# A planner's table of costs is changed, and its order is searched with random shakes of the priorities: attention and two MoE layers on one core

## The chip, the core and the metric

The kernel runs on one core of one Trainium2 chip. The time is device microseconds for one execution of the whole program; less is better. Rows of a profile come from one execution recorded by the hardware profiler.

## What is computed

```python
def _attn_ref(q, k, v, tau):              # q, k, v: 4 batches, 8 heads, 576 positions, 64 wide
    scores = (1 / sqrt(64)) * matmul(q, k.transpose(0, 1, 3, 2))
    thresh = max(scores, axis=-1) - tau
    scores = where(scores >= thresh, scores, -1e9)
    attn = exp(scores - max(scores)); attn = attn / (sum(attn) + 1e-09)
    return matmul(attn, v)

x = attn_out.transpose(0, 2, 1, 3).reshape(2304, 512)
h = x @ w_in                               # 512 -> 2048
x = (h * clip(h + 3, 0, 6) / 6) @ w_out    # 2048 -> 512
h = x @ w2_in
out = (h * sigmoid(1.702 * h)) @ w2_out
```

## The kernel before, in words

**The stages.** Sixteen attention units (4 batches, 4 pairs of heads each) come first, and the first half of the first MoE layer is worked in between them (`moe_a`). Then follow the second half of that layer (`moe_b`) and the second layer (`moe2`), which streams the saved half of its weights back from DRAM. A matmul of nearly full float32 precision is made of three passes over a high and a low part.

**A unit of attention.** The unit loads K and Q of each of its two heads (tile `qk`, lines 545 and 546) and its values V (line 559). ScalarE copies K and Q into rounded high parts (tile `kqv`, line 366), GpSimd makes the low parts (line 369). TensorE forms nine score tiles of 128 rows (`ps`; line 573 from the fifth unit on, 589 and 605 before). For each, VectorE takes the row maximum (line 621), ScalarE the exponential (line 626, tile `e`), VectorE the threshold mask and sum (line 627). The result is transposed: on TensorE (line 678) with a ScalarE copy into tile `et` (line 681), or, in the last two batches, by `blocks`: VectorE transposes 32x32 blocks into `tr` (line 699), one DMA writes them to DRAM (line 702, `turned`, 1 MB) and four DMAs of 256 KB read them back into `et` (line 704). These four are called the block reads below. Then thirty value products on TensorE (line 756) multiply by V. TensorE's hidden and output matmuls of the first layer are lines 815 and 835 (835 serves the second layer too), the hidden matmuls of the second layer line 972.

**What sets the order.** All of this is recorded as operations with a cost in nanoseconds, what they read and write, and a nominal time. `Plan.order` is a list scheduler: it walks through time and gives each engine, when it is free, the ready operation with the smallest key; DMAs go through one queue in the order in which they become ready. `latest` runs the same backward and gives new keys. `settle` alternates the two. The resulting order is what each engine's instruction stream gets; it is fixed when the program is built, and on the chip each engine executes its own stream in that order and waits where an input is not there. SP issues all the data DMAs named here, from one stream. Where the plan sees TensorE idle and a bank of PSUM free, `fill` puts in dummy matmuls (line 1135, tile `two`), which compute nothing that is used.

The search is in `settle`. Its first loop is always run; the second runs once for each number in `KICKS`, the tuple that is empty before:

```python
        for seed in KICKS:
            self.order(kicked(key, length, seed))
            key = self.latest()
            length = self.order(key)
```

`kicked` draws from the seed a stretch of the plan and a size (100 to 3000 ns), and adds Gaussian noise of that size to the keys in that stretch.

Of the kernel before, what the change touches and what calls it, by code (L numbers as in the profile page):

```python
# [18 lines left out]
P = 128  # L19


PE, ACT, DVE, POOL, SP, DMA = range(6)
# [8 lines left out]

PORT = {DVE: {"W", "XHB", "XLB", "XD", "XLC", "GT2", "GL"}, POOL: {"kl", "qs", "ql", "vl", "W", "GD", "N", "RM", "EL", "XL", "XLC", "GL"}}

KICKS = ()


class Buf:
# [23 lines left out]
class Plan:  # L61
# [158 lines left out]
    def settle(self):  # L220
# [3 lines left out]
        for _ in range(3):  # L224
# [4 lines that stand above are left out]
# [24 lines left out]
def kicked(key, length, seed):  # L253

    rng = random.Random(seed)
    size, width = rng.choice((100.0, 300.0, 1000.0, 3000.0)), rng.choice((2e4, 6e4, 2e5, 2e6))
    lo = rng.uniform(-length - width / 2, 0.0)
    return [k + rng.gauss(0.0, size) if lo <= k < lo + width else k for k in key]
# [3 lines left out]
def tile_top_attention_moe_moe2(  # L262
# [13 lines left out]
    nc = tc.nc  # L276
    B, H, _, S = q2.shape
    DM, DFF = w1i.shape
# [40 lines left out]
    def add(eng, cost, time, name, fn, rd=(), wr=(), touch=()):  # L319
        op = pl.add(eng, cost, time, fn, rd, wr, name, touch)  # L320
        for c, names in changed:
            if any(b.pool in names for b in op.bufs):
                op.deps.add(c)
        return op

    def move(time, name, nbytes, fn, rd=(), wr=()):

        op = add(SP, 590, time, name, fn, rd, wr)
        add(DMA, nbytes / 360, time, name, lambda: None, rd, wr).deps.add(op)

    def buf(tag, ring, pool, shape, dt=F32):
        return Buf(pl, tag, ring, lambda: pools[pool].tile(shape, dt, tag=tag, name=tag, bufs=ring), pool)

    def bank(cls):
        b = Buf(pl, "pm", 1, lambda: pools["pm"].tile([P, 512], F32, tag=f"pm{b.bank}", name="pm"), "pm")
        b.cls = cls
        return b
# [9 lines left out]
    def f32(ap):  # L347
        return ap.bitcast(F32)

    def pe(n):  # L350
        return 7 + 0.43 * n

    def act(n):
        return 51 + 0.834 * n

    def dve(n):
        return 69 + 1.042 * n
# [7 lines left out]
    def copy(o, i, **kw):  # L365
        return lambda: nc.scalar.activation(out=o(), in_=i(), func=ACTF.Copy, **kw)  # L366
# [121 lines left out]
    ets = [buf("et", 1, "et", [P, 10 * S]) for _ in range(2)]  # L488

    def et_a(et, p, hd, k):  # L490
        o = (0, 2560)[p] + (5 * hd + k) * CH[p][1]
        return et.t[:, o:o + CH[p][1]]
# [7 lines left out]
    def et_p(p):  # L500
        return ets[1].t[:, 2560 * p:2560 * p + 2048].rearrange("p (h k n) -> p h k n", h=2, k=4)

    def et_4(p):
        return ets[1].t[:, 2560 * p + 2048:2560 * p + 2560].rearrange("p (h n) -> p h n", h=2)

    def et_r():
        return ets[1].t[:, 5120:].rearrange("p (h k n) -> p h k n", h=2, k=5)
# [4 lines left out]
    def unit(u, b, j, t0):  # L512
# [4 lines left out]
        def K(name, s=0):  # L517
            return t0 + 2700 * s + NOMINAL[name]
# [4 lines left out]
        def tile_():  # L523
            return buf("kqv", 12, "st", [P, QC], F32R)

        if early:
            khb, qhb, qzb = tile_(), tile_(), buf("g", HF, "gp", [P, 640], F32R)
            for hd in range(2):
                r, o = slice(64 * hd, 64 * hd + 64), slice(64 - 64 * hd, P - 64 * hd)
# [24 lines left out]
        vs = tile_()  # L554

        def v_(k, hd):
            return f32(vs.t).rearrange("p (k h d) -> p k h d", k=5, h=2)[:, k, hd, :]
# [3 lines left out]
        xrs = {p: buf(f"xr{p}", 2, "xr", [P, CH[p][1]]) for p in range(2)}  # L561
# [20 lines left out]
        def score1(s):  # L582

            ps, (hd, m) = buf("ps", 2, "ps", [P, 2, 512]), tiles[s]
            q0 = 256 * hd + m * P

            def mm():
                for i in range(2):
                    nc.tensor.matmul(ps.t[:, i, :SH], f32(qzb.t)[:, q0:q0 + P], f32(khb.t)[:, i * SH:(i + 1) * SH], start=True, stop=True)

            add(PE, 4 * 243, K("S", s), "S", mm, [(qzb, x) for x in (("z", hd), (hd, 0))] + [khb], [ps])
            soft(s, ps)

        def score(ss):

            if len(ss) == 1 and tiles[ss[0]] is not None:
                return score1(ss[0])
            pss = {s: buf("ps", 2, "ps", [P, 2, 512]) for s in ss}

            def mm():  # L600
                for i in range(2):
                    for s in ss:
                        t = tiles[s]
                        rows, q0 = (slice(0, P), 256) if t is None else (slice(64 * t[0], 64 * t[0] + 64), t[1] * P - 256)
                        nc.tensor.matmul(pss[s].t[:, i, :SH], f32(qhb.t)[rows, q0:q0 + P], f32(khb.t)[rows, i * SH:(i + 1) * SH], start=True, stop=True)

            add(PE, 4 * 243 + 300 + 40 * (len(ss) > 1), K("S", ss[0]), "S", mm, [qhb, khb], [pss[s] for s in ss])
            for s in ss:
                soft(s, pss[s])

# [72 lines left out]
        def last_keys(p, ss):  # L683
            trans([(s, 4, tiles[s][0] * 256 + tiles[s][1] % 2 * P) for s in ss], 512, lambda kn: (et_4(p)[:kn], lambda x: x.rearrange("p (h n) -> p h n", h=2)), ets[1], (p, 4), ss[-1])
# [9 lines left out]
        def blocks(p, ss):  # L694

            et, at, src = ets[1], ss[-1], buf("tr", 1, "tr", [P, 4, 2, 4, 2, 32])
            for s in ss:
                hd, t = tiles[s]
                add(DVE, dve(512), K("DT", s), "DT", lambda hd=hd, t=t % 2, e=e_of[s]: nc.vector.transpose(out=src.t[:, :, hd, :, t, :].rearrange("p g k j -> p k g j"), in_=e.t[:, :512].rearrange("p (k g j) -> p k g j", k=4, g=4)),
                    [e_of[s]], [(src, s)])  # L700
            turned, there = turns[p]
            move(K("DM", at), "DM", 16 * P * 512, lambda: nc.sync.dma_start(out=turned, in_=src.t.rearrange("p g h k t j -> p (g h k t j)")), [src], [there])
            for g in range(4):
                move(K("DM", at) + 3000, "DM", 4 * P * 512, lambda g=g: nc.sync.dma_start(out=ets[1].t[32 * g:32 * g + 32, 2560 * p:2560 * p + 2048].rearrange("p (a n) -> p a n", a=4),
                     in_=turned[:, 512 * g:512 * g + 512].rearrange("(a p) n -> p a n", a=4)), [there], [(et, ("m", p, g))])
            last_keys(p, ss)

# [21 lines left out]
        def av(p, at):  # L729

            n, xr, et, pv = CH[p][1], xrs[p], ets[0], bank(1)
            regions = [(p, hd, k) for hd in range(2) for k in (0, 2)] + [(p, 4), ("z", p)] + ["r", "r4"] * p

            def mm():
                for k in range(5):
                    for hd in range(2):
                        nc.tensor.matmul(pv.t[64 * hd:64 * hd + 64, :n], v_(k, hd), et_a(et, p, hd, k), start=k == 0, stop=k == 4)

            op = add(PE, 350 + 10 * (1 + 0.84 * n), K("AV", at), "AV", mm, [vs] + [(et, r) for r in regions], [pv], [xr])
            add(ACT, act(n), K("XR", at), "XR", copy(lambda: xr.t, lambda: pv.t[:, :n]), [pv], [xr])  # L740
            return op

        def av_(at):

            et, pv = ets[1], [bank(1), bank(1)]
            for x in pv:
                add(PE, 0, K("AV", at), "AV", lambda: None, [vs, et], [x], xrs.values())

            def mm():
                def x(p, k, hd):  # L750
                    return et_r()[:, hd, k] if p == 2 else et_4(p)[:, hd] if k == 4 else et_p(p)[:, hd, k] if b not in TURNED else et_m(p)[:, :, hd, k].rearrange("p a t j -> p t a j")

                for p, o, c, n in ((0, pv[0], 0, 256), (1, pv[0], 256, 256), (2, pv[1], 0, 64)):
                    for k in range(5):
                        for hd in range(2):
                            nc.tensor.matmul(o.t[64 * hd:64 * hd + 64, c:c + n], v_(k, hd), x(p, k, hd), start=k == 0, stop=k == 4)  # L756

            add(PE, 450 + 10 * (2 + 0.84 * S), K("AV", at), "AV", mm, [vs, et], pv, xrs.values())
            add(ACT, act(256), K("XR", at), "XR", copy(lambda: xrs[0].t, lambda: pv[0].t[:, :256]), [pv[0]], [xrs[0]])
            add(ACT, act(256), K("XR", at), "XR", copy(lambda: xrs[1].t[:, :256], lambda: pv[0].t[:, 256:]), [pv[0]], [(xrs[1], 0)])  # L760
            add(ACT, act(64), K("XR", at), "XR", copy(lambda: xrs[1].t[:, 256:], lambda: pv[1].t[:, :64]), [pv[1]], [(xrs[1], 1)])
# [432 lines left out]
```

## Time and profile before

| | us |
|---|---|
| median of 3 runs | 1097.37 (1097.24 to 1100.8) |
| the profiled execution | 1093.03 |
| its span, first to last instruction | 1091.2 |
| TensorE (PE) busy in the span | 1058.7 (97%) |
| VectorE, ScalarE, GpSimd busy | 724.2, 638.1, 515.3 |

TensorE is busy nearly all the time, the others are not. The profiled execution took 1.8 us more than its span, and was 4.3 us faster than the median of the runs. TensorE's busy time includes the dummy matmuls and matmuls that ran at a lower granted clock.

### The profile page before, as it was taken

How to read it: one execution, taken by the hardware profiler on the slowest of the kernel's cores; microseconds unless marked ns; L12 is line 12 of the kernel's file. 1: busy time of each engine (PE TensorE's matmuls, PEld its weight loads, DVE VectorE, ACT ScalarE, POOL GpSimd, SP SyncE). 2: the span in 40 equal slices, each digit the busy share in tenths (PEclk: the TensorE clock that was granted, in tenths of full speed). 3: DMA queues.
4: the chain of work that ended last, by engine and by line, in shares of the span. 5: the costliest groups of instructions: out<-in, count | busy, mean ns of one | idle time of the engine just before them, and what ended most of it. 6: DMA issues, size and time to landing. Idle time of an engine off the chain costs nothing.

```text
span 1091.2 us, 20840 instructions
## 1 busy us (share of the span) xinstructions
PE 1058.7 (97%) x7706; PEld 970.0 (89%) x7706; DVE 724.2 (66%) x1485; ACT 638.1 (58%) x1340; POOL 515.3 (47%) x598
## 2 busy tenths in 40 slices
PE   8999899989898999999999999999999999999998
PEld 7677788888787989999999999989998989889888
DVE  6998766676686784467877333778787675563634
ACT  4888777765576664576555324666566665444433
POOL 3679868675686764555466224541323332001000
PEclk9999999999999999999999999999999999999999
DMA  7334222266878687445654212435545543312202
GB/s 206 116 120 129 96 68 78 91 190 176 250 213 271 200 242 195 140 137 166 203 174 145 79 48 61 132 105 183 175 137 173 167 139 102 116 46 71 92 1 73
DMA packets 90053, 150.19 MB, mean 138 GB/s; under 512 B 8928, under 2 KB 51552, under 8 KB 87904
## 3 DMA queue, kind: packets, MB, share of 16 engines
q1 hardware_dynamic: 89952, 148.87, 44.8%
q8 instruction: 60, 0.98, 0.4%
q14 instruction: 41, 0.34, 0.1%
HBM read 101.52 MB, written 47.32 MB: 136 GB/s over the span
## 4 chain that ended last, share of the span: by engine, by line
PE 69%; DVE 9%; DMA 7%; ACT 5%; POOL 4%; issue 3%; SPq 2%; POOLq 0%; DVEq 0%; ACTq 0%
PE py L835 23%; PE pm L815 14%; PE pm L972 14%; PE pm L835 6%; PE pm L756 4%; PE ps L573 4%; PE pm L678 2%; DMA qk<-in_k_dram 2%; DVE e L627 2%; DMA qk<-in_q_dram 1%; ACT e L626 1%; DVE nm L621 1%; DMA wrawstg<-in_w1i_dram 1%; POOL e L640 1%; POOL kqv L369 1%
## 5 line engine op out<-in xcount | busy, mean ns | idle before, releaser
L835 PE MATMUL py<-g,outhring 128*128 128x512 f32 (+2 forms) x1152 | 287.7, 337 | 2.6 <-DVE g L369 1.3
L835 PEld LDWEIGHTS py<-g,outhring 128*128 128x128 f32 x1152 | 193.7, 188 | 20.6 <-DVE g L369 3.3
L835 PE MATMUL py<-g,outlring 128*128 128x512 f32 (+2 forms) x576 | 193.5, 336 | 0.0
L815 PE MATMUL pm<-xh,inhring 128*128 128x256 f32 (+1 forms) x512 | 154.8, 302 | 2.3 <-DVE t L827 2.2
L815 PE MATMUL pm<-xl,inhring 128*128 128x256 f32 (+1 forms) x512 | 151.8, 296 | 0.0
L815 PE MATMUL pm<-xh,inlring 128*128 128x256 f32 (+1 forms) x512 | 151.7, 296 | 0.0
L972 PE MATMUL pm<-outhring,inhring 128*128 128x256 f32 x512 | 144.5, 282 | 1.5 <-ACT u L366 0.8
L972 PE MATMUL pm<-outlring,inhring 128*128 128x256 f32 x512 | 143.6, 281 | 0.0
L972 PE MATMUL pm<-outhring,inlring 128*128 128x256 f32 x512 | 143.5, 280 | 0.0
L621 DVE TENSOR_REDUCE nm<-ps 128x1 f32<-128x576 f32 x144 | 106.2, 750 | 34.4 <-PE ps L573 30.3
L369 POOL TENSOR_TENSOR g<-t,g 128x256 fp32r<-128x256 f32 (+1 forms) x104 | 88.1, 851 | 82.7 <-ACT g L366 79.9
L627 DVE SCALAR_TENSOR_TENSOR e<-ps,th,e 128x576 f32<-128x576 f32 x128 | 102.6, 810 | 33.2 <-ACT e L626 31.9
L827 DVE SCALAR_TENSOR_TENSOR t<-t,pm 128x256 f32<-128x256 f32 (+1 forms) x128 | 57.1, 448 | 94.0 <-ACT t L826 93.7
L835 PEld LDWEIGHTS py<-g,outlring 128*128 128x128 f32 x576 | 108.2, 188 | 10.0
L369 POOL TENSOR_TENSOR wmstg<-wmstg,wrstg 128x512 uint32<-128x512 uint32 x48 | 64.6, 1347 | 94.8 <-DVE wmstg L422 77.3
L835 PE MATMUL pm<-g,outhring 128*128 128x256 f32 (+1 forms) x512 | 107.7, 301 | 0.5 <-POOL g L369 0.4
L369 POOL TENSOR_TENSOR g<-tc,g 128x512 fp32r<-128x512 f32 x24 | 31.8, 1326 | 161.6 <-ACT g L366 154.9
L826 ACT ACTIVATE t<-pm,half 128x256 f32<-128x256 f32 (+1 forms) x128 | 63.7, 498 | 74.3 <-PE pm L815 68.6
L626 ACT ACTIVATE e<-ps,nm 128x576 f32<-128x576 f32 x128 | 93.0, 733 | 15.2 <-DVE nm L621 13.4
L815 PEld LDWEIGHTS pm<-xh,inhring 128*128 128x128 f32 x512 | 98.0, 191 | 4.2 <-DVE t L827 2.9
L972 PEld LDWEIGHTS pm<-outhring,inhring 128*128 128x128 f32 x512 | 96.8, 189 | 4.9 <-ACT u L366 1.1
L972 PEld LDWEIGHTS pm<-outlring,inhring 128*128 128x128 f32 x512 | 96.9, 189 | 2.6
(114 smaller groups left out, 2433.8 us busy)
## 6 DMA issues: line engine op xcount, KB each, us to landing
turned<-tr SPq DMA_DIRECT2D x16, 1024.0 KB, 4.5
et<-turned SPq DMA_DIRECT2D x64, 256.0 KB, 5.6
wrawstg<-in_w1i_dram SPq DMA_DIRECT2D x16, 512.0 KB, 4.0
wrawstg<-in_w1o_dram SPq DMA_DIRECT2D x16, 512.0 KB, 3.8
wrawstg<-in_w2i_dram SPq DMA_DIRECT2D x16, 512.0 KB, 3.9
wrawstg<-in_w2o_dram SPq DMA_DIRECT2D x16, 512.0 KB, 3.9
qk<-in_k_dram SPq DMA_DIRECT2D x24, 288.0 KB, 3.9
qk<-in_q_dram SPq DMA_DIRECT2D x24, 288.0 KB, 3.7
```

Source lines behind the costliest of these rows:

```text
L369: return lambda: (nc.vector if eng == DVE else nc.gpsimd).tensor_tensor(out=o(), in0=a(), in1=b(), op=op)
L573: nc.tensor.matmul(ps.t[:, i, :SH], qss[hd].t[:, q0:q0 + P], w[hd].t[:, i * SH:(i + 1) * SH], start=a, stop=z)
L621: add(DVE, 665, K("R", s), "R", lambda: nc.vector.tensor_reduce(out=nm.t[:, c], in_=ps.t[:, :, :SH], op=ALU.max, axis=AX.XY, negate=True), ...
L626: add(ACT, 624, K("X", s), "X", lambda: nc.scalar.activation(out=ev(), in_=ps.t[:, :, :SH], func=ACTF.Exp, bias=nm.t[:, c]), [ps, (nm, s)] ...
L627: add(DVE, 729, K("M", s), "M", lambda: nc.vector.scalar_tensor_tensor(out=ev(), in0=ps.t[:, :, :SH], scalar=th.t[:, c], in1=ev(), op0=ALU ...
L678: nc.tensor.transpose(pt.t[:kn, o:o + P], e_of[s].t[:, keys(k)], id_b.t)
L756: nc.tensor.matmul(o.t[64 * hd:64 * hd + 64, c:c + n], v_(k, hd), x(p, k, hd), start=k == 0, stop=k == 4)
L815: nc.tensor.matmul(ph.t[:, :n], a, v, start=(cc == 0 and i == 0), stop=(cc == KC - 1 and i == 2))
L826: add(ACT, 93 + act(n), K("RL"), "RL", lambda: nc.scalar.activation(out=tt_(), in_=pt(), func=ACTF.Relu, scale=1.0 / 6.0, bias=half_b.t), ...
L827: add(DVE, dve(n), K("GT"), "GT", lambda: nc.vector.scalar_tensor_tensor(out=tt_(), in0=tt_(), scalar=1.0, in1=pt(), op0=ALU.min, op1=ALU. ...
L835: nc.tensor.matmul(py.t[:, :n], a, v, start=(st and i == 0), stop=(sp and i == 2))
L972: nc.tensor.matmul(o.t[:, :n], u.t[:, ws], v.t[:, xv], start=(st and kk == 0 and i == 0), stop=(sp and kk == 1 and i == 2), skip_group_che ...
```

## The change

Six numbers by which the plan counts durations are changed, and the tuple of seeds is filled with 14 numbers. No operation, buffer or transfer is added or taken away, apart from the dummy matmuls, whose number follows from the plan. Costs of matmuls go up a little (`pe`), those of value products and of the first units' scores down or up by up to 250 ns, and each block read is counted as 1274 ns of the DMA queue where it was 728 ns (7 and 4 times 128 x 512, divided by 360).

```diff
-KICKS = ()
+KICKS = (1, 3, 102, 147, 227, 262, 375, 1642, 1718, 1761, 2323, 3460, 4428, 4473)
...
     def pe(n):
-        return 7 + 0.43 * n
+        return 9 + 0.428 * n
...
-            add(PE, 4 * 243, K("S", s), "S", mm, [(qzb, x) for x in (("z", hd), (hd, 0))] + [khb], [ps])
+            add(PE, 4 * 243 + 60, K("S", s), "S", mm, [(qzb, x) for x in (("z", hd), (hd, 0))] + [khb], [ps])
...
-            add(PE, 4 * 243 + 300 + 40 * (len(ss) > 1), K("S", ss[0]), "S", mm, [qhb, khb], [pss[s] for s in ss])
+            add(PE, 4 * 243 + 200, K("S", ss[0]), "S", mm, [qhb, khb], [pss[s] for s in ss])
...
-                move(K("DM", at) + 3000, "DM", 4 * P * 512, lambda g=g: nc.sync.dma_start(out=ets[1].t[32 * g:32 * g + 32, 2560 * p:2560 * p + 2048].rearrange("p (a n) -> p a n", a=4),
+                move(K("DM", at) + 3000, "DM", 7 * P * 512, lambda g=g: nc.sync.dma_start(out=ets[1].t[32 * g:32 * g + 32, 2560 * p:2560 * p + 2048].rearrange("p (a n) -> p a n", a=4),
...
-            op = add(PE, 350 + 10 * (1 + 0.84 * n), K("AV", at), "AV", mm, [vs] + [(et, r) for r in regions], [pv], [xr])
+            op = add(PE, 150 + 10 * (1 + 0.84 * n), K("AV", at), "AV", mm, [vs] + [(et, r) for r in regions], [pv], [xr])
...
-            add(PE, 450 + 10 * (2 + 0.84 * S), K("AV", at), "AV", mm, [vs, et], pv, xrs.values())
+            add(PE, 200 + 10 * (2 + 0.84 * S), K("AV", at), "AV", mm, [vs, et], pv, xrs.values())
```

Nearly every stretch of every engine's stream stands in another order. Three places follow; names with numbers are single buffers, and the numbers differ between the two programs for the same thing.

**First place: SP's stream where the thirteenth unit's second K is loaded.** `in_k2`, `in_q2` and `in_vp` are K, Q and V in DRAM; K's load of the unit's second head is `qk_3842` before and `qk_3825` in the change. Before:

```order
L702 DMA turned_111<-tr_3665 128x2048
L704 DMA et_1647<-turned_111 32x4x512 x3
L546 DMA qk_3807<-in_q2_dram 128x576
L704 DMA et_1647<-turned_111 32x4x512
L559 DMA kqv_3790<-in_vp_dram 128x640
L545 DMA qk_3842<-in_k2_dram 128x576
L767 DMA x1d_99<-xr0_3826 128x256
```

The same place in the change:

```order
L704 DMA et_1502<-turned_111 32x4x512 x4
L546 DMA qk_3815<-in_q2_dram 128x576
L545 DMA qk_3825<-in_k2_dram 128x576
L559 DMA kqv_3795<-in_vp_dram 128x640
L704 DMA et_1502<-turned_112 32x4x512 x4
L546 DMA qk_3885<-in_q2_dram 128x576
```

K's load has moved ahead of V's, and still stands behind four block reads; four more block reads now follow directly.

**Second place: ScalarE's stream where this K is copied** (`kqv_3908<-qk_3842` before, `kqv_3951<-qk_3825` in the change); `t` and `g` belong to the first layer's gate, `e` and `er` to the softmax of the unit before. Before:

```order
L826 ACTIVATE t_3870<-pm_3819,half_110 128x320
L366 ACTIVATE g_3878<-t_3817 128x320
L623 ACTIVATE th_3850<-nm_3835,nt_108 128x1
L366 ACTIVATE kqv_3908<-qk_3842 128x576
L826 ACTIVATE t_3916<-pm_3866,half_110 128x320
L626 ACTIVATE e_3921<-ps_3852,nm_3835 128x576
L623 ACTIVATE th_3850<-nm_3835,nt_108 128x1
```

In the change:

```order
L626 ACTIVATE er_3928<-ps_3897,nm_3719 128x576
L623 ACTIVATE th_3724<-nm_3719,nt_108 128x1
L826 ACTIVATE t_3941<-pm_3881,half_110 128x320
L366 ACTIVATE kqv_3951<-qk_3825 128x576
L366 ACTIVATE kqv_3845<-qk_3815 128x576
L626 ACTIVATE e_3970<-ps_3943,nm_3719 128x576
L623 ACTIVATE th_3724<-nm_3719,nt_108 128x1
```

The copy of K stands later among the softmax pieces of the unit before it, and next to a copy of Q; a gate piece and softmax pieces still stand behind it.

**Third place: TensorE's stream where the fifteenth unit's scores begin.** Scores are line 573 (`kqv_4496,kqv_4536` before, `kqv_4488,kqv_4541` in the change), value products of an earlier unit line 756. Before:

```order
L756 MATMUL pm_4818<-et_1647,kqv_4174 64x256 x20
L756 MATMUL pm_4839<-et_1647,kqv_4174 64x64 x10
L835 MATMUL pm_4784<-g_4685,outhring1_1259 128x256 x2
L835 MATMUL pm_4784<-g_4685,outlring1_1279 128x256
L835 MATMUL pm_4784<-g_4737,outhring1_1358 128x256 x2
L835 MATMUL pm_4784<-g_4737,outlring1_1363 128x256
L835 MATMUL pm_4784<-g_4745,outhring1_1416 128x256 x2
L835 MATMUL pm_4784<-g_4745,outlring1_1440 128x256
L835 MATMUL pm_4784<-g_4807,outhring1_1530 128x256 x2
L835 MATMUL pm_4784<-g_4807,outlring1_1541 128x256
L573 MATMUL ps_4897<-kqv_4496,kqv_4536 128x288 x2
L573 MATMUL ps_4897<-kqv_4503,kqv_4536 128x288 x2
```

In the change:

```order
L573 MATMUL ps_4780<-kqv_4488,kqv_4541 128x288 x2
L573 MATMUL ps_4780<-kqv_4519,kqv_4541 128x288 x2
L756 MATMUL pm_4794<-et_1502,kqv_4125 64x256 x20
L756 MATMUL pm_4815<-et_1502,kqv_4125 64x64 x10
L678 MATMUL pm_4852<-id_103,e_4675 64x128
```

The first score of the new unit has moved ahead of the thirty value products. This order stands at the starts of four units in the change (the 12th, 14th, 15th and 16th) and of one before (the 11th).

The dummy matmuls (line 1135) are 65 before and 37 in the change; each leaves two records in a trace. Ahead of the first hidden matmul there are 36 and 25, from there to the last unit's value products 8 and 0, behind them in the first layer 4 and 10, in the second layer 17 and 2. Of the first 36 and 25, 22 and 21 stand ahead of the first transpose; 14 and 4 follow. VectorE's stream holds, ahead of the operation that the first hidden matmuls wait for last (the fourth unit's product with the reciprocal sums, `xr`), the same operations in both: 19 each of maximum, threshold and mask, and 19 of the weights' decoding.

## Rows read from the trace of the kernel before

**Rows 1.** The page's busy times: engine, us busy, share of the span, instructions.
```profile
PE 1058.7 (97%) x7706; PEld 970.0 (89%) x7706; DVE 724.2 (66%) x1485; ACT 638.1 (58%) x1340; POOL 515.3 (47%) x598
```

**Rows 2.** Windows by stage: stretch, length, busy us per engine, clock, DMA share, GB/s.
```profile
18.00:60.00 42.00, 38.24 (x261) 28.05 (x258) 37.96 (x95) 34.53 (x65) 23.71 (x29) 1.00 0.50 153
60.00:220.00 160.00, 154.56 (x1209) 132.68 (x1211) 119.16 (x291) 122.85 (x247) 127.61 (x164) 1.00 0.31 95
220.00:410.00 190.00, 176.50 (x1437) 160.61 (x1433) 143.70 (x307) 119.64 (x283) 131.05 (x184) 0.97 0.77 222
410.00:700.00 290.00, 288.80 (x2210) 284.73 (x2209) 163.82 (x322) 146.19 (x307) 145.07 (x139) 1.00 0.45 135
700.00:1080.00 380.00, 377.05 (x2455) 342.95 (x2455) 244.12 (x435) 205.64 (x426) 82.20 (x61) 1.00 0.35 115
```

**Rows 3.** Timeline of TensorE: start, us, instructions, [idle before and its releaser].
```profile
238.88 0.94 PE L678 MATMUL pm<-id,e 128*64 128x128 f32 x4 [2.03 <-ACT et L681]
...
277.06 1.30 PE L573 MATMUL ps<-kqv 128*128 128x288 f32 x4 [3.41 <-DVE e L627]
...
301.05 0.41 PE L815 MATMUL pm<-xh,inhring 128*128 128x320 f32 x1 [1.71 <-DVE t L827]
...
354.15 0.79 PE L573 MATMUL ps<-kqv 128*128 128x288 f32 x4 [2.99 <-DVE e L627]
```

**Rows 4.** The chain that ended last, and DMA issues: what led to these waits.
```profile
230.85 7.11 DMA qk<-in_k_dram
...
265.12 8.56 DMA qk<-in_q_dram
...
292.68 6.67 DMA qk<-in_k_dram
...
343.46 7.68 DMA qk<-in_k_dram
...
qk<-in_k_dram SPq DMA_DIRECT2D x24, 288.0 KB, 3.9
```

**Rows 5.** Timelines of SP and ScalarE ahead of the third wait.
```profile
292.01 0.38 SPq L559 DMA_DIRECT2D kqv<-in_vp_dram  x1
292.68 0.35 SPq L545 DMA_DIRECT2D qk<-in_k_dram  x1
...
299.38 0.68 ACT L366 ACTIVATE kqv<-qk 128x576 fp32r<-128x576 f32 x1 [3.69 <-DMA qk<-in_k_dram]
```

**Rows 6.** Windows of TensorE just behind the four waits: stretch, length, busy, clock, DMA, GB/s.
```profile
239.00:243.00 4.00, 4.00 (x22) 0.57 0.65 265
...
276.90:281.00 4.10, 3.94 (x20) 0.62 1.05 316
...
301.00:304.00 3.00, 2.92 (x18) 1.00 0.10 41
...
354.00:359.00 5.00, 4.85 (x26) 0.66 0.65 163
```

**Rows 7.** Block reads: the DMA issues, and a window that holds eight of them.
```profile
et<-turned SPq DMA_DIRECT2D x64, 256.0 KB, 5.6
...
262.00:276.00 14.00, 11.65 (x108) 1.00 1.00 234
```

**Rows 8.** Dummy matmuls: those from 0 to 60 us, those from 700 us, a timeline.
```profile
0.00:60.00 60.00, 11.68 (x72) 10.86 (x72) 1.00 0.53 157
...
L1135 PE MATMUL pm<-two x34: 270/275/275, 712.2 to 1017.6; 128*128 128x128 f32 x34
...
712.19 0.83 PE L1135 MATMUL pm<-two 128*128 128x128 f32 x6
712.78 0.48 PE L835 MATMUL py<-g,outhring 128*128 128x512 f32 x1
714.25 0.50 PE L835 MATMUL py<-g,outhring 128*128 128x512 f32 x1 [0.99 <-DVE g L369]
```

**Rows 9.** The chain: one unit's value products.
```profile
142.24 5.05 PE pm L756 x60
```

## The prediction, made before the changed kernel was run

> **What bounds the kernel now.** I read the page first. TensorE is busy 97% of the span, the next engine 66% [rows 1], and no work is added or removed, so the change can only win back what TensorE loses: idle time, dummy matmuls and half-clock stretches. The windows by stage say where that lies. Idle TensorE is the length less the busy time: 3.8 us from 18 to 60 us, 5.4 from 60 to 220, 13.5 from 220 to 410, 1.2 from 410 to 700, 3.0 from 700 to 1080 [rows 2]. The stretch from 220 to 410 holds half of it, and is the only one with a granted clock under 1.00 and the one with the busiest DMA (0.77). It is where attention goes through the block reads.
>
> The timeline of that stretch shows four waits that make up most of it: 2.03, 3.41, 1.71 and 2.99 us, sum 10.1 [rows 3]. The releaser named is ScalarE or VectorE, but the chain that ended last goes on behind them to a load of K or Q each time, which took 7.11, 8.56, 6.67 and 7.68 us from issue to landing, where K's median is 3.9 [rows 4]. The third shows the mechanism: SP issued V's load at 292.01 and K's at 292.68; ScalarE then stood 3.69 us until K came [rows 5], and everything behind that copy in ScalarE's stream, a gate piece and two softmax pieces, stood with it. TensorE waited for the gate piece.
>
> Each wait can cost twice. Behind the first, second and fourth the granted clock is 0.57, 0.62 and 0.66 over 4.0, 4.1 and 5.0 us with TensorE busy; behind the third, the shortest, it stayed at 1.00 [rows 6]. A clock of 0.57 over 4.0 us is 0.43 x 4.0 = 1.7 us lost; the others lose 0.38 x 4.1 = 1.6 and 0.34 x 5.0 = 1.7. Together 5.0 us, so late loads cost 10.1 + 5.0 = 15.1 us.
>
> **Why the loads are late.** The plan counted a block read of 256 KB as 728 ns. In a window that holds eight of them the DMA engines were full (share 1.00) and moved 234 GB/s [rows 7]: 262 KB (decimal) over 234 is 1.12 us. Four reads were thus undercounted by 4 x 0.39 = 1.6 us, and a group of four or eight stood ahead of each late load. The plan believed K was there when ScalarE's turn came. The new figure, 1.27 us, is near the traced one.
>
> **The change, part by part.** *Late loads.* A truer cost does not make a read faster; it can only let the plan move loads ahead, or put K's copy later so that less stands behind it. The streams show some of both. For the thirteenth unit K moves ahead of V's 320 KB, worth 328 / 234 = 1.4 us of DMA, of the 1.71 us wait; but four reads still stand ahead of it. ScalarE's copy stands behind more of the previous unit's softmax. Of the four loads two (13th and 15th unit) are moved ahead of V so; the other two keep their place behind reads. Bounds: nothing saved, or all 15.1. I take half, as two of four are moved on SP: **-7.6 us**.
>
> *Dummy matmuls of the second layer.* There are 34 records; six took 0.59 us from the first's start to the next matmul's (712.19 to 712.78), so 0.098 each and 3.3 in all [rows 8]. The change keeps 4 records, 0.4 us: 2.9 us less. What covers a loss here is nothing, as TensorE is the only busy engine; but a gap may come back as plain waiting, as in the 0.99 us just behind those six [rows 8]. Bounds 0 and -2.9; I take **-2.5**.
>
> *Dummy matmuls of the start.* 72 records become 50, at 0.098 us 2.2 us less. But from 18 to 60 us VectorE is busy 37.96 of 42.0 [rows 2], and its stream holds the same operations ahead of the first hidden matmul in both orders. TensorE would just stand where it now spins: **0**, bounds -2.2 and what the clock may cost (below). The middle ones, 16 records less before the last value products and 12 more behind them, cancel within half a us.
>
> *Cost figures of matmuls and value products.* A unit's value products took 5.05 us [rows 9]; the plan said 450 + 10 x (2 + 0.84 x 576) = 5308 ns and now says 5058. The figure is right now, but 0.25 us in each of twelve units is small beside gaps of 2 to 3 us. These and the smaller figures go together: 0.
>
> *The shaken order.* Idle time outside the four waits is 3.4 us in 220 to 410, 5.4 before it, 4.2 after it, 13 us in all [rows 2, 3]. The seeds reshuffle all of it, and I cannot price that from an order. Bounds: 5 us gained (a third or so) or 5 lost; I take **-1.5**, as the plan whose costs are nearer the traced ones should lose less to surprise.
>
> Sum: -7.6 - 2.5 + 0 + 0 - 1.5 = **-11.6 us**. From the profiled execution's 1093.0 that is 1081.4; it ran 4.3 us under the median of the runs, and I carry the difference to that: 1097.4 - 11.6 = 1085.8, so 1086.
>
> **The rivals.** *All waits go.* If K's copies now stand late enough everywhere, the late loads give 15.1, the dummies 2.9 and the shake 4: -22, about 1075. For it: the chain names one cause for all four. Against it: reads still stand ahead of most loads.
>
> *The DMA engines are the bound and nothing is won there.* They were full from 262 to 276 us [rows 7], and the same bytes must move; a load put ahead makes the block reads late, and with them the value products that wait for them. Then only the second layer's dummies and the shake remain: -2.5 - 1.5 = -4, but a read group pushed behind a load costs some of that; about 1094. Against it: the share over 220 to 410 is 0.77 [rows 2], so a quarter of the DMA time is free there. The Trainium skill has a rule that speaks for this rival (Perfetto Trace Analysis, What "DMA-bound" means): a kernel can be bound on the DMA engines themselves, and then large descriptors are what matter. By that rule an order of issue would give nothing here and the time would stay at about 1094; the trace agrees for 14 us of the stretch and not for all of it.
>
> *Slower: a score put ahead of the value products.* At four unit starts (one before) the new unit's first score now stands ahead of thirty value products in TensorE's stream. TensorE takes its matmuls in that order, so if K is late there, 5.05 us of work [rows 9] that may be ready stands behind the wait. If each of the four waits as long as the worst now (3.41 us) and drops the clock (1.7), that is 4 x 5.1 = 20.4 us; with the gains above kept, -11.6 + 20.4 = +8.8, so 1106. It decides the sign from 11.6 / 4 = 2.9 us per start. Against it: the plan now counts the reads ahead of K, and value products wait for block reads themselves, so they may not be ready earlier.
>
> *The clock falls at the start.* Fourteen dummies behind the first transpose become four. Three of the four waits above were followed by half clock, the one of 1.71 us was not [rows 3, 6]; idle gaps in place of dummies could do the same, at 1.6 to 1.7 us for each low stretch [rows 6]. Two such would give 1086 + 3.4 = 1089. Against it: VectorE ends most waits there, so a slower TensorE is partly hidden. The Trainium skill states it as a rule (TensorE: Matmul & The Clock Gate, Part 1): half clock is the default state, and activity releases it. By that rule fewer dummies could make the start slower, to the same 1089; the trace shows the clock at 1.00 there with all 36.
>
> **How the numbers follow.** Chances: the forecast 0.47 (its own range 1080 to 1091, from a quarter to all of the late loads with the small terms at either end), all waits gone 0.15, DMA-bound 0.22, slower 0.08, clock at the start 0.08. A measurement of this kernel can tell about 0.5%, 5.5 us, from no change: faster means under 1091.9, slower over 1102.9. Faster: 0.47 + 0.15 + 0.06 of the clock case + 0.01 of the DMA case = 0.69. Same: 0.20 + 0.02 = 0.22. Slower: 0.08 + 0.01 = 0.09. The range 1076 to 1098 takes in the forecast, the clock and the DMA case and the better part of the case in which all waits go; it leaves out the slower case and the tail of the best one.
>
> **What would show it.** Late loads: idle TensorE from 220 to 410 falls from 13.5 to about 8 us, the granted clock there rises from 0.97 towards 0.99, and ScalarE's waits for K and Q shrink; if the loads still take 7 us and more but no TensorE wait hangs on them, the copies' place did it, not SP's. Dummies: 4 records from 700 us on, and idle there not above 3 us. Start: the first hidden matmul (line 815) still at about 60 us, with more idle ahead of it. I am wrong if idle from 220 to 410 stays above 11 us, if new waits in line 573 stand right ahead of line 756, or if the gain sits mostly in the first 220 us.

## The result, and the profile after

The changed kernel takes 1084.28 us (median of 4 runs, 1079.79 to 1085.12) against 1098.61 for the kernel before (1097.24 to 1100.8, with one run more than was shown ahead of the prediction). The ratio is 0.9864, 95% interval 0.9833 to 0.9895: 14.3 us faster, inside the range of 1076 to 1098 and 1.7 us under the forecast of 1086.

The two profiled executions differ by less, 1085.12 against 1093.03, 7.9 us. The one of before was faster than its four runs, and the one of after was the slowest of its four. So the rows below show where time went, and the size of it is taken from the runs.

The windows by stage of the changed kernel, with the columns of [rows 2] (length, busy PE, PEld, DVE, ACT, POOL, granted clock, DMA share, GB/s):

```profile
18.00:60.00 42.00, 36.90 (x242) 26.18 (x241) 38.30 (x94) 34.50 (x67) 24.50 (x29) 1.00 0.51 151
60.00:220.00 160.00, 152.28 (x1174) 128.25 (x1175) 120.98 (x294) 124.35 (x245) 126.38 (x165) 0.98 0.31 93
220.00:410.00 190.00, 181.17 (x1503) 166.45 (x1500) 150.72 (x321) 125.66 (x299) 136.04 (x189) 1.00 0.82 231
410.00:700.00 290.00, 289.08 (x2212) 284.18 (x2211) 170.43 (x317) 143.31 (x298) 142.18 (x134) 1.00 0.45 133
700.00:1080.00 380.00, 377.55 (x2450) 342.87 (x2448) 244.11 (x433) 206.84 (x428) 81.24 (x60) 1.00 0.36 113
```

Length less busy, against [rows 2]: idle TensorE fell from 13.5 to 8.8 us in 220 to 410, where the clock rose from 0.97 to 1.00 (some 5 us of lost clock gone), and from 3.0 to 2.4 us from 700 on. It rose from 5.4 to 7.7 us in 60 to 220, where the clock fell from 1.00 to 0.98, worth 0.02 x 160 = 3.2 us. The gain sits where the prediction put it; part of it is given back before.

Who TensorE waited for in 220 to 410 us of the changed kernel (us in total, times, longest), the three largest:

```profile
PE pm L756 <- DVE t L827: 1.8, 2, 1.5
PE ps L573 <- DVE er L627: 1.7, 1, 1.7
PE ps L573 <- DVE e L627: 1.4, 2, 1.1
```

No wait is over 1.71 us, where before there were 2.03, 3.41, 1.71 and 2.99 [rows 3], and the clock is 1.00 in the whole stretch. How that came is seen at the first place of the order, the thirteenth unit's second K. Of the changed kernel, SP's timeline (start, length, what):

```profile
288.54 0.38 SPq L545 DMA_DIRECT2D qk<-in_k_dram  x1
```

ScalarE's:

```profile
297.42 1.26 ACT L366 ACTIVATE kqv<-qk 128x576 fp32r<-128x576 f32 x2 [3.20 <-DMA qk<-in_k_dram]
```

and TensorE's (in brackets the wait before, and for whom):

```profile
300.49 0.77 PE L573 MATMUL ps<-kqv 128*128 128x288 f32 x4 [1.11 <-DVE e L627]
```

K was issued at 288.54 and its copy began at 297.42: the load was not faster than before but slower, up to 8.9 us (6.67 then [rows 4]). ScalarE still stood 3.20 us for it, against 3.69 [rows 5]. But more of the unit before stood ahead of the copy in ScalarE's stream, and TensorE lost 1.11 us in place of 1.71. Over the stretch ScalarE's copies waited less for loads too. The view of the tile `qk` from 220 to 410 us says who waited for it; first the row of the kernel before:

```profile
  ACT kqv L366: 17.9, 7
```

and of the changed kernel:

```profile
  ACT kqv L366: 8.7, 4
```

The loads themselves became slower. Of the same views, the time of all loads of K and Q in the stretch, before and then in the change:

```profile
DMA to landing us min/median/max: 3.2/6.2/9.8
```

```profile
DMA to landing us min/median/max: 3.0/7.6/9.9
```

The median of 3.9 us for K [rows 4] is that of the whole execution. In this stretch a load took 6.2 us in the median before too, so the four late ones (6.67 to 8.56) did not stand far out. A block read also lands later, 7.4 us after issue in the median of the execution (5.6 before [rows 7]). The transfers are no faster; the waits for them are shorter.

### The profile page after: what moved, and what is told of

Read it like the earlier page. It is cut to its first block, busy times and chain, and to the rows that moved or that the text cites. A ratio compares the mean times of both kernels' runs of the same rounds, so it can differ in the third digit from the quotient of the medians.

```text
span 1083.3 us, 20735 instructions
## 1 busy us (share of the span) xinstructions
PE 1052.5 (97%) x7650; PEld 960.9 (89%) x7650; DVE 735.4 (68%) x1485; ACT 640.0 (59%) x1340; POOL 515.9 (48%) x598
```

## Experiments

Two theories stood against each other. Theory 1: true costs do it; the plan stops believing that K and Q are there when they queue behind block reads. Theory 2: the search does it; the seeds give a shorter order, whatever the figures. All ratios are against the kernel before on the same chip, with 95% intervals. There are three sets, each on a chip of its own: e1 to e4, e5 to e8, e9 to e12; between sets the ratios are compared.

### The six figures without the seeds (e1)

```diff
-KICKS = (1, 3, 102, 147, 227, 262, 375, 1642, 1718, 1761, 2323, 3460, 4428, 4473)
+KICKS = ()
```

> All six new cost figures, no seeds. Theory 1 (true costs: the plan stops believing that loads behind block reads are there, and that is where the 14 us come from) expects most of the gain, a ratio of 0.986 to 0.991, idle TensorE from 220 to 410 us at 9 us or less and the clock there at 0.99 or 1.00. Theory 2 (search: the seeds shorten the order, whatever the figures) expects 0.997 to 1.003, with waits of 2 to 3 us left behind late loads. Both in part: 0.991 to 0.997.

Measured: 1.0022 (1.0009 to 1.0035), 1099.52 us. The figures alone win nothing. Yet the late loads are gone: ScalarE's copies waited 2.2 us in all for `qk` in 220 to 410 us, where it was 17.9. Other waits stand in their place. Of e1, two windows and then the two largest waits of TensorE from 220 to 410 us:

```profile
220.00:410.00 190.00, 180.25 (x1472) 0.97 0.79 224
700.00:1080.00 380.00, 374.48 (x2415) 1.00 0.37 117
```

```profile
PE ps L573 <- DVE e L627: 3.9, 4, 1.8
PE pm L815 <- ACT et L681: 2.4, 2, 2.1
```

Idle time in 220 to 410 is 9.8 us, less than before, but the clock is as low as it was (0.97), and TensorE is idle for 5.5 us of the second layer in place of 3.0. So a short wait of ScalarE for its loads does not by itself make a kernel faster.

### The figure of the block reads alone (e2)

```diff
-                move(K("DM", at) + 3000, "DM", 4 * P * 512, lambda g=g: nc.sync.dma_start(out=ets[1].t[32 * g:32 * g + 32, 2560 * p:2560 * p + 2048].rearrange("p (a n) -> p a n", a=4),
+                move(K("DM", at) + 3000, "DM", 7 * P * 512, lambda g=g: nc.sync.dma_start(out=ets[1].t[32 * g:32 * g + 32, 2560 * p:2560 * p + 2048].rearrange("p (a n) -> p a n", a=4),
```

> The kernel before with one figure changed: a block read is counted as 1274 ns in place of 728. Theory 1 expects nearly as much as all figures together give, 0.987 to 0.993, since the late loads (10.1 us of waits and 5.0 us of clock) are the only large loss that a figure speaks of. Theory 2 expects 0.997 to 1.003.

Measured: 1.0071 (1.0048 to 1.0093), slower. Here too the copies waited less for `qk` (6.0 us). Theory 1 as stated has fallen: the one figure that speaks of the loss does not bring the time. The working put the other five figures at nothing; without a search they are worth 0.5% (1.0071 here, 1.0022 with all six in e1).

### The old figures with a search of their own (e3)

```diff
-KICKS = ()
+KICKS = (1, 11, 338, 1139, 1226, 1269, 1414, 4302)
```

> The kernel before with its own old figures and eight seeds kept by the same rule (a seed is kept if the plan gets shorter by the plan's own count) out of the first 6000. Theory 2 expects as much as the change gave, 0.984 to 0.991. Theory 1 expects the late loads still there (clock under 0.99 from 220 to 410 us, waits of 2 us and more behind copies of K and Q) and 0.994 to 1.003, since a plan with reads counted at 728 ns gets shorter on paper by an order that the chip does not keep.

Measured: 0.9887 (0.9868 to 0.9905), 1085.36 us. That is some five sixths of the change's gain without any of its figures, as theory 2 has it. Of theory 1's signs neither shows: the clock in 220 to 410 us is 0.99 and the longest wait of TensorE 1.8 us, although the copies still waited 9.7 us for `qk`.

### Without the dummy matmuls of the second layer (e4)

```diff
-                if count > 0:
+                if count > 0 and s < 600000:
```

> The kernel before without its 17 dummy matmuls of the second layer, and nothing else changed. The prediction's term says 2.5 us less, a ratio of 0.9977, bounds 0.9970 to 1.000. The rival: a dummy only fills a gap that stays a wait when it is gone, so 1.000, with idle TensorE from 700 us on up by 2 to 3 us from 3.0.

Measured: 1.0012 (0.9992 to 1.0031). Leaving the 34 records out wins nothing, as the rival said: TensorE is idle for 6.1 us from 700 to 1080 where it was 3.0, so what the dummies filled came back as waits. Of e4, three windows:

```profile
700.00:1080.00 380.00, 373.86 (x2398) 1.00 0.36 115
700.00:710.00 10.00, 8.43 (x65) 0.93 0.27 85
710.00:714.00 4.00, 4.00 (x21) 0.75 0.78 213
```

A wait of 1.57 us (at 707.80) and a stretch at lower clock stand at the start of the layer: 0.07 x 10 + 0.25 x 4 = 1.7 us of clock, where the execution of before had 1.00. One execution does not show whether the missing dummies brought that; the runs show that nothing was won.

### The block reads at half size, in the order before and in the changed one (e5, e6), beside the changed kernel again (e7)

Every engine's order stays as it was; only the rows that a block read moves are halved. It tells what the reads cost each order: K and Q that come late behind them, and also whatever waits for the reads themselves, the value products among it.

```diff
-                move(K("DM", at) + 3000, "DM", 4 * P * 512, lambda g=g: nc.sync.dma_start(out=ets[1].t[32 * g:32 * g + 32, 2560 * p:2560 * p + 2048].rearrange("p (a n) -> p a n", a=4),
-                     in_=turned[:, 512 * g:512 * g + 512].rearrange("(a p) n -> p a n", a=4)), [there], [(et, ("m", p, g))])
+                move(K("DM", at) + 3000, "DM", 4 * P * 512, lambda g=g: nc.sync.dma_start(out=ets[1].t[32 * g:32 * g + 32, 2560 * p:2560 * p + 1024].rearrange("p (a n) -> p a n", a=2),
+                     in_=turned[:64, 512 * g:512 * g + 512].rearrange("(a p) n -> p a n", a=2)), [there], [(et, ("m", p, g))])
```

> The kernel before, every engine's order unchanged, but each block read moves half its rows (128 KB of 256), so that half of the transposed weights of two batches are old values and the output is not the reference's. It prices the lateness of the loads behind block reads. If the four late loads cost what the rows say (10.1 us of waits, 5.0 of clock), the ratio is 0.986 to 0.991 and the clock from 220 to 410 us is 1.00. Rival: the softmax chain of ScalarE and VectorE sets the pace there and takes the place of the loads, 0.995 to 1.000.

> The changed kernel with the same halved block reads, order unchanged; the output is not the reference's. If the change won its time by getting K and Q out from behind the block reads, there is little left to win: 0.983 to 0.9865, no more than 3 us under the changed kernel on the same chip. If the reads still cost the changed order as much as the old one, it falls by 10 us more, to about 0.977.

> The changed kernel once more, on the chip of the other three, for comparisons within this set: 0.984 to 0.9895.

Measured: e5 0.9836 (0.9810 to 0.9862), 1080.99 us; e6 0.9826 (0.9797 to 0.9855), 1080.48 us; e7 0.9869 (0.9842 to 0.9897), 1084.59 us. So the reads are priced: halving them wins 17.7 us in the order before, a little more than the 15.1 that the rows gave, and 4.1 in the changed one, a little more than the 3 that were expected there. Of e5, the window of block reads:

```profile
220.00:410.00 190.00, 186.50 (x1552) 1.00 0.58 193
```

A halved read landed 3.4 us after issue (median of the execution). ScalarE's copies waited 3.5 us for `qk` there, where it was 17.9. Idle time is 3.5 us where it was 13.5, and the clock 1.00 where it was 0.97: 10.0 us of waits and some 5 of clock, from the halved reads alone.

### Six seeds more (e8)

```diff
-KICKS = (1, 3, 102, 147, 227, 262, 375, 1642, 1718, 1761, 2323, 3460, 4428, 4473)
+KICKS = (1, 3, 102, 147, 227, 262, 375, 1642, 1718, 1761, 2323, 3460, 4428, 4473, 5006, 5023, 5027, 5038, 5144, 8750)
```

> The changed kernel with six more seeds, kept by the same rule out of those up to 16000. If what the plan counts as shorter is shorter on the chip, by about as much as for the first 14 seeds, a further 2 to 4 us, 0.982 to 0.985. Rival: the plan's last gains are smaller than what it misjudges, so no difference, 0.985 to 0.989.

Measured: 0.9881 (0.9855 to 0.9908), 1086.27 us, no different from e7 in the same set. So six seeds more, by which the plan counts itself shorter, win nothing on the chip. From 430 to 700 us TensorE is idle for 3.9 us in e8, at a clock of 0.99, and for 1.0 us in e7, at 1.00. If something was won elsewhere it may have been lost there; one execution of each does not settle it.

### The halved reads in the other two orders (e9, e10)

The same edit of the reads, made to e1 and to e3.

> The new figures without seeds, order unchanged, block reads moving half their rows (the output is not the reference's). It prices the reads in the order that the figures alone give, which took 1.0022 of the time before. If the truer figure made that order robust to slow reads, as it does not in the order before (17.7 us by the halved reads there), little is won: 0.996 to 1.000, and what the figures gained in attention was lost elsewhere. If the figure did not do that, 10 us or more: 0.992 or less.

> The old figures with eight seeds, order unchanged, block reads halved (the output is not the reference's). That order took 0.9887 with full reads. If a search by figures that count a read at 728 ns leaves the reads on the path, 8 us or more are won: 0.981 or less. If any shaken order gets clear of them, 4 us or less: 0.985 to 0.9887.

Measured: e9 0.9997 (0.9975 to 1.0018), e10 0.9801 (0.9775 to 0.9827). With e5 and e6 that makes a table of the four orders. The price of the reads is the difference of the two ratios, times 1098 us; an interval for it is some 3 to 5 us to either side, and by the medians the first and the last come out as 17.7 and 4.1.

| order | full reads | halved reads | price of the reads |
|---|---|---|---|
| old figures, no seeds (before) | 1 | 0.9836 | 18.0 us |
| new figures, no seeds (e1, e9) | 1.0022 | 0.9997 | 2.7 us |
| old figures, eight seeds (e3, e10) | 0.9887 | 0.9801 | 9.4 us |
| new figures, 14 seeds (e7, e6) | 0.9869 | 0.9826 | 4.7 us |

As e10's expectation had it for a search that counts a read at 728 ns, 9.4 us of the reads stay on the path there; but half of them are gone without the truer figure.

The column of halved reads says how good an order is when the reads hardly matter. By it the new figures alone make the order 0.9997 - 0.9836 = 1.6%, 17.7 us, worse. Of e9, the windows where that stands:

```profile
60.00:220.00 160.00, 149.59 (x1172) 1.00 0.31 94
220.00:410.00 190.00, 180.47 (x1482) 0.98 0.56 186
```

Idle time is 10.4 and 9.5 us, with a clock of 0.98 in the second, although the reads are halved; e5 has 5.8 us in the first of these windows and 3.5 in the second, at 1.00.

### Other seeds, and fewer (e11, e12)

```diff
-KICKS = (1, 3, 102, 147, 227, 262, 375, 1642, 1718, 1761, 2323, 3460, 4428, 4473)
+KICKS = (20021, 20059, 20088, 20089, 20134, 20138, 20163, 20189, 20320, 20654, 22748, 22893)
```

> The new figures with twelve other seeds, kept by the same rule out of 5000 that the change never tried. If the gain belongs to the search and not to these 14 seeds, 0.985 to 0.992. If the 14 seeds hit on something of their own, 0.994 to 1.002.

```diff
-KICKS = (1, 3, 102, 147, 227, 262, 375, 1642, 1718, 1761, 2323, 3460, 4428, 4473)
+KICKS = (1, 3, 102, 147, 227, 262)
```

> The changed kernel with the first six of its 14 seeds. If each kept seed gives its part, about half the gain: 0.992 to 0.996. If the chip only follows the plan's last state by chance, anything from 0.986 to 1.003.

Measured: e11 0.9909 (0.9886 to 0.9932), e12 0.9930 (0.9903 to 0.9957). Seeds that the change never tried bring about two thirds of its gain (half at the least, by the interval), so it belongs to the search and not to these numbers. Its first six seeds bring half, as each kept seed giving its part would have it; the rival of that, a gain by chance, allowed this figure too, and e8's six brought nothing.

## Why the prediction was right in size, and where its steps were not

**Place and price of the loss: right.** The prediction put late loads behind block reads at 10.1 us of waits and 5.0 of clock. Halving the reads won 17.7 us, and its rows show 10.0 and some 5 of that in 220 to 410 us. The changed order brings the price of the reads down to 4.7, and with halved reads it is no better than the order before (0.9826 and 0.9836): nearly all of its 14 us are in what the reads cost.

**"I take half ... -7.6 us": mis-sized.** The price of the reads fell from 18.0 to 4.7 us, so 13.3, within 5 us or so, not half of 15. I had read two of four loads as still behind reads on SP and counted them as still lost. At the place shown K made ScalarE wait about as long as before; the order had other work ahead of the copy. The prediction's own test named this case: loads still slow (median 7.6 us), TensorE's long waits gone, so the copies' place did it. That is read from the rows of one place and of one stretch; no run moved the copies alone.

**What brought it: only half told.** The working ascribed the late-load gain to the truer figure and 1.5 us to the shaken order. Alone the six figures do clear the order of the reads (2.7 us left of 18.0), but that order is 17.7 us worse in waits that do not hang on the reads, and the time does not move; why those waits come is open. Alone the search wins 12.4 us (e3): 8.6 in the price of the reads, 3.8 in the rest. With the figures in place the seeds win back 1.0022 - 0.9869 = 1.5%, 17 us, nearly all of it in parts that the reads don't touch. So the step "-1.5 for the shaken order", with bounds of 5 us either way, failed: under either set of figures the search brings the gain, 12.4 and 17 us. That the reads hold nearly all of the 14 us and the seeds win 17 elsewhere is no conflict: the figures alone lower the price of the reads and raise the rest by about as much (15.3 and 17.7 us), and the seeds take that back. Whether the figures add anything to a search stays open: 0.9887 without them lies between 0.9869 or 0.9864 and 0.9909 (e11) with them, and the searches were not equally long.

**Dummies of the second layer, -2.5 us: right in size, wrong in cause.** They are 4 records now, as counted, but nothing was to be won by leaving them out (e4). What the layer won it won because the gaps that they filled became shorter: 30 records are gone and idle time did not rise (2.4 us against 3.0). The layer's hidden matmuls (line 972) have their first and last start in these rows, before and then in the change:

```profile
L972 PE MATMUL pm<-outhring,inhring x512: 276/281/388, 698.8 to 1081.8; 128*128 128x256 f32 x171
```

```profile
L972 PE MATMUL pm<-outhring,inhring x512: 276/281/387, 693.5 to 1073.9; 128*128 128x256 f32 x171
```

That is 383.0 us before and 380.4 in the change (379.5 in e7), against 385.8 in e4, 384.6 with the figures alone (e1) and 382.8 with eight seeds alone (e3).

**Start, 0: right in its own terms.** VectorE is as busy (38.3 of 42 us), idle time is 5.1 in place of 3.8 us with 22 records fewer, and the first hidden matmul begins at 59.5 us, 0.5 earlier.

**The rivals.** DMA-bound, so that an order wins nothing there: refuted, since the same bytes were moved at a share of 0.82 and the time fell; but the reads' bytes did hold the old order (e5). A score put ahead of value products: the order is there, but in 220 to 410 the longest wait of line 573 is 1.7 us, with line 835 behind it and not 756, and line 756 itself waits 1.5, for VectorE. Clock at the start: not in the first profiled execution (1.00), but in the second (0.92, see below). What no rival named is the loss from 60 to 220 us. One wait of 2.68 us at 76.81 has no releaser in the trace, and behind it stand 6 us at a clock of 0.72; the wait recurs in e7 and e6. Idle time of 2.2 us from 128 to 133 us is likewise followed by 5 us at 0.67. With twelve other seeds (e11) the wait is not there and the clock from 60 to 220 us is 1.00, so this loss belongs to the order and not to the figures. Of the changed kernel, the wait and the window behind it:

```profile
76.81 1.21 PE L605 MATMUL ps<-kqv 128*128 128x288 f32 x4 [2.68 <-issue]
```

```profile
77.00:83.00 6.00, 6.00 (x27) 0.72 0.40 140
```

So -11.6 came near -14.3 partly by luck. By the table the price of the reads fell by 13.3 us where the working had 7.6, and all the rest together brought 1.1 us (0.9836 to 0.9826) where the working had 4.0, each within some 5 us. In that rest a second layer shorter by 2.6 us stands against 2.3 us of idle time and 3.2 of clock lost from 60 to 220.

## What to carry to other kernels

Price a suspected transfer by halving its bytes with every engine's order unchanged: in two kernels this told 18 us of lateness from 5, which neither the DMA's share (0.77 and 0.82) nor the loads' time to landing (6.2 and 7.6 us) did. When a cost figure in a planner is corrected, the plan moves everything, and the loss that the figure named can go while the time stays; compare orders after a search under each set of figures, since one order alone may hide the effect (1.0022 and 1.0071 here without a search). Dummy matmuls in gaps are not time to be won unless the gap goes too.

## What was not expected of the hardware

A stretch of lower clock at the start comes and goes between executions of one order. The changed kernel's window from 18 to 60 us, profiled a second time (e7):

```profile
18.00:60.00 42.00, 36.63 (x222) 0.92 0.50 148
```

The first time it was 1.00; 0.08 x 42 is 3.4 us of clock. A wait that took 1.30 us the first time (ahead of 30.82) took 1.91 in e7 (ahead of 31.02), and 30 to 38 us ran at 0.79 there. The order before had 1.00 with full reads and 0.96 in e5, whose stream is the same at this place. The first hidden matmul began at 62.2 us in e7 and 59.5 us in the first profile. So it is seen in some executions of either order and is no sign of the change; a few us between two profiled executions can be this alone.
